# Two streamed weight granules of the last projection phase, 41 and 44, trade places with their neighbours 42 and 45

## The chip, the cores and the metric

The kernel runs on one core of a Trainium2 chip. The metric is the device time of one execution in microseconds (us); of several executions the median is given. Beside the times there is one profiled execution, whose page and trace are quoted here. Engines are called as the profile calls them: PE is TensorE, DVE is VectorE, ACT is ScalarE, POOL is GpSimd, SP is SyncE.

## The reference: what is computed

The input x is 2048 rows of 1024 values in bfloat16. It is normalised row by row (xn), and the output is x plus two terms.

The first term is a recurrent attention. The 2048 rows are cut into 64 segments of 32 rows. Each segment is put behind an 8-row memory, so 40 rows go through q, k and v projections (1024 to 32 heads of 128), masked softmax attention and the output projection:

```python
h = jnp.concatenate([mem, xs], axis=1)          # 8 memory rows, 32 rows of the segment
q = jnp.einsum('btd,dhe->bhte', h, Wq)          # likewise k and v
...
o = jnp.einsum('bhte,hed->btd', o, Wo)
mem = o[:, :M, :].copy()                        # the memory of the next segment
outs.append(o[:, M:, :])
```

The memory of a segment is made by the one before it, so the segments run one after the other, and each needs all of Wq, Wk, Wv and Wo.

The second term is a router that picks two of the 2048 rows and runs them through a gated feed-forward layer (1024 to 3584 and back); the result is added to these two rows.

## The kernel before, in words

**Weights and granules.** The four matrices of the attention are cut into 64 granules of 128 x 2048 values (512 KB). Granules 0 to 47 belong to six projection phases of eight granules each, in the order of the list `PHASES` (L25): q and k of the first half of the heads, q and k of the second half, then v of the first half (granules 32 to 39) and v of the second half (granules 40 to 47). Granules 48 to 63 are the output projection. 44 granules stay resident on the chip; the other 20 are streamed from HBM again in every segment, each into one of five slots (`wstream`, `N_SLOT`, L19 and L97). Which ones are streamed is the list `streamed` (L74 to L80). In the kernel before it holds 2, 5, 6, 9, 13, 17, 21, 25, 29, 33, 36, 39, 41, 44, 47, 50, 53, 56, 59 and 62. After the first segment granule 6 is no longer read and only half of granule 25 is (the rest is kept in PSUM), so 19 reads remain per segment. In the first segment GpSimd copies the streamed granules to a scratch tensor in HBM (`wsc`), from which later segments read.

**The stream.** `fetch` (L318) issues the next read of a fixed list on SyncE's queue; later segments use the line L327. It needs a free slot, so SyncE waits until TensorE has finished with the slot's last content. Fetches are issued in order, five granules ahead: what frees a slot is that all matmuls of a streamed granule are done, and `after` (L434), called at that point of the program, issues the next fetch. So the end of streamed granule number n in the list is followed by the fetch of number n + 5: the end of 41 by the fetch of 56, the end of 44 by that of 59.

**The order of work.** The order on each engine is written out by hand; no scheduler changes it. Per segment TensorE runs the six phases (loop at L650), in each phase the eight granules in order, each with four matmuls 128*32 by 512 columns (L668, tile `PSm`). Between granules stand hooks, small pieces of other work tied to a phase and a granule: the transposes of the projections, `scores` (L527), the softmax on ScalarE and VectorE, and `attend` (L571, matmuls at L583 and L585). The first `attend` of the first half stands behind the fifth granule of the last phase (granule 44), the second one behind the seventh (granule 46). ScalarE copies its result (L590 and L592). Then come the 16 granules of the output projection (`project`, L722), with the `attend` of the second half between them.

**The left rows.** The main pass of a segment takes 32 of its 40 rows: 24 of x and the 8 of the memory. The last 8 rows of x of four successive segments (a group) are handled together, as 32 left rows. Their projections are passes of their own over the same granules (`left_pass`, L644 to L647, tile `PSl`, four more matmuls per granule). They are spread over the group by j, the number of a segment in its group: in segments j = 1 and j = 2 those of q and k of the next group, in segments j = 0 those of v, in the two v phases; segments j = 3 have the output projection of the left rows (tile `WL`). Where the phase before had left passes too, the left passes of the first three granules of a phase are put behind the main pass of the fourth, and `after` is called behind the left pass:

```python
if PSl is None or kc >= 3 or not left_before:
    for g_, Gv_ in behind:
        if PSl is not None and g_ not in done and g_ not in later:
            left_pass(PSl, g_, Gv_, not done and g_ == rest[0], g_ == rest[-1])
        after(s, g_)
    behind = []
```

In segments j = 0 this concerns the second v phase, with granules 40, 41 and 42. For q and k of the second half the passes over resident granules are put off further (the list `later`); this does not apply to v.

**The rest.** GpSimd's queue carries the rows of x, the outputs and the left rows; ScalarE's queue stores the left projections (`ql_d`). At the end the weights of the feed-forward layer are read into the places of granules that are no longer needed (L371).

Of the kernel before, what the change touches and what calls it, by code (L numbers as in the profile page):

```python
# [17 lines left out]
N_RES = 44  # L18
N_SLOT = 5  # L19
KEPT_WHOLE = 6  # L20
KEPT_PART = 25
LEFT_OUT = 35
NEG = -30000.0

PHASES = [(0, 0), (1, 0), (0, 1), (1, 1), (2, 0), (2, 1)]  # L25
# [3 lines left out]
def kernel(  # L29
# [41 lines left out]


    NG = 64
    n_str = NG - N_RES  # L74
    streamed = [((2 * i + 1) * NG) // (2 * n_str + 2) for i in range(n_str + 1)]
    streamed.remove(LEFT_OUT)

    moved = {1: 2, 4: 5, 7: 9, 10: KEPT_WHOLE, 16: 17, 19: 21, 22: KEPT_PART, 25: 29, 28: 33, 32: 36, 38: 39}
    streamed = sorted(moved.get(g, g) for g in streamed)
    resident = [g for g in range(NG) if g not in streamed]  # L80

    def granule_dram(g):
# [417 lines left out]
    for s in range(NSEG):  # L500
# [149 lines left out]
        for p, (mat, half) in enumerate(PHASES):  # L650
# [13 lines left out]
            for kc in range(KC):  # L664
                g = 8 * p + kc
# [255 lines left out]
```

## Time and profile before

| | |
|---|---|
| Runs of the kernel before | 1920.88, 1941.53 and 1932.7 us, median 1932.7 |
| The profiled execution's own time | 1935.58 us |
| Its span, first to last instruction | 1933.6 us |
| Mean granted TensorE clock in it | 0.957 of full speed |
| DMA packets | 712.42 MB, mean 368 GB/s |

The span is what the profile's shares refer to. A row of a group or of the timeline names a line of the kernel, an engine, an operation and the tile it writes, then `<-` and what it reads: `PSm<-g,ST` is a main matmul with a streamed granule (g) and the segment's rows (ST), `PSm<-wres,ST` one with a resident granule. A timeline row gives start and length in us, counts like instructions in a row (x4) and, in brackets, how long the engine had been idle before it and what ended that. The ends of matmuls are modelled and overlap the next ones, so the time that a granule takes is read from start to start. A row of a table by windows gives the stretch, its length, each engine's busy time and instructions, the granted clock, the share of DMA busy time and GB/s.

### The profile page before, as it was taken

Reading aid. Unit: us, or ns where it says so; the run is one execution under the profiler, and the core shown is the slowest. Engines: PE = TensorE matmul, PEld = TensorE weight load, DVE = VectorE, ACT = ScalarE, POOL = GpSimd, SP = SyncE. Lnnn points to the kernel's source line nnn. Section 1 sums busy time; section 2 is a strip of 40 time slices with the busy share of each in tenths; the row PEclk is TensorE's granted clock in tenths of the full one; section 3 lists DMA queues with packets and bytes.
Section 4 is the critical chain, followed back from the end, with each engine's and each line's share of the span. In section 5 each row is a group of like instructions: output and inputs, shape, how many; then the busy total and the mean of one; then the engine's idle time right before and its main releaser. Section 6 shows DMA issues by size and latency. Waiting matters only on the chain.

```text
span 1933.6 us, 82883 instructions
## 1 busy us (share of the span) xinstructions
PE 1619.9 (84%) x36080; PEld 883.4 (46%) x36080; DVE 887.4 (46%) x2848; ACT 721.0 (37%) x1931; POOL 439.9 (23%) x882
## 2 busy tenths in 40 slices
PE   3558898989889898989999898988889898988874
PEld 1224444445444444445454444545444554545443
DVE  6734543554444445444454454444444444345430
ACT  1124343444434343433444343443434343344320
POOL 3211212222221312222131221222131222212120
PEclk8669999999999999999999999999999999999985
DMA  9999999999999999999999999999999999999998
GB/s 369 408 356 379 344 375 352 378 376 362 379 330 387 367 372 388 355 371 341 379 375 379 370 382 358 357 389 357 378 362 368 377 370 373 352 382 362 375 370 334
DMA packets 232123, 712.42 MB, mean 368 GB/s; under 512 B 39296, under 2 KB 53168, under 8 KB 231760
## 3 DMA queue, kind: packets, MB, share of 16 engines
q1 hardware_dynamic: 194384, 671.18, 92.3%
q0 software_dynamic: 28736, 28.09, 4.4%
q10 hardware_dynamic: 8640, 7.87, 1.2%
q8 instruction: 282, 4.62, 0.9%
q14 instruction: 81, 0.66, 0.1%
HBM read 694.32 MB, written 22.29 MB: 371 GB/s over the span
## 4 chain that ended last, share of the span: by engine, by line
PE 45%; DMA 44%; DVE 4%; ACT 3%; issue 3%; SPq 0%; ACTq 0%; POOL 0%; POOLq 0%; DVEq 0%
DMA g<-wsc 38%; PE PSm L668 22%; PE WO L722 7%; PE PSl L646 4%; PE BT L515 3%; PE WL L722 3%; ACT OTL L592 1%; PE BT L465 1%; DMA MW<-in_B_w_gate_dram 1%; DVE XR L227 1%; DMA MW<-in_B_w_up_dram 1%; DMA g<-in_A_Wq_dram 1%; DMA wres<-in_A_Wo_dram 1%; PE BS L583 1%; ACT QT L520 1%
## 5 line engine op out<-in xcount | busy, mean ns | idle before, releaser
L668 PE MATMUL PSm<-wres,ST 128*32 128x512 bf16 x8448 | 720.1, 386 | 18.2 <-DVE ST L282 6.7
L668 PEld LDWEIGHTS <-ST 128*32 128x32 bf16 x12288 | 324.1, 96 | 418.1 <-issue 191.3
L668 PE MATMUL PSm<-g,ST 128*32 128x512 bf16 x3588 | 365.5, 387 | 97.0 <-DMA g<-wsc 78.3
L684 ACT CAST XB<-PSm 128x512 bf16<-128x512 f32 x256 | 149.8, 585 | 293.8 <-PE PSm L668 292.3
L722 PEld LDWEIGHTS <-OT 128*32 128x32 bf16 x8192 | 202.4, 97 | 105.4 <-issue 84.5
L722 PE MATMUL WO<-wres,OT 128*32 128x256 bf16 x5632 | 231.9, 277 | 18.9 <-issue 9.6
L458 POOL DMA_DIRECT2D LX<-ql_d x63 | 33.5, 532 | 876.4 <-DVE OTL L592 350.8
L646 PE MATMUL PSl<-wres,STL 128*32 128x512 bf16 x2112 | 196.6, 390 | 2.5 <-issue 1.6
L525 DVE COPY KT<-BT 128x512 bf16<-128x512 bf16 x128 | 52.5, 410 | 313.7 <-ACT XB L684 134.5
L252 POOL DMA_DIRECT2D XN<-in_A_x_dram x256 | 128.5, 507 | 242.1 <-DMA out_dram<-XN 106.4
L786 POOL DMA_DIRECT2D out_dram<-XN x256 | 129.1, 513 | 222.0 <-DVE XN L784 216.1
L722 PE MATMUL WO<-g,OT 128*32 128x256 bf16 x2560 | 131.3, 279 | 37.3 <-DMA g<-wsc 29.2
L706 ACT CAST VM<-PSm 128x512 bf16<-128x512 f32 x128 | 79.7, 623 | 123.1 <-PE PSm L668 123.1
L520 ACT COPY QT<-BT 128x512 bf16<-128x512 bf16 x128 | 74.9, 585 | 113.0 <-PE BT L515 111.9
L646 PEld LDWEIGHTS <-STL 128*32 128x32 bf16 x3072 | 85.0, 98 | 63.9 <-issue 11.5
L350 ACT COPY BK<-KEPT 128x512 bf16<-128x512 bf16 x126 | 78.3, 621 | 90.8 <-PE WO L722 90.8
L354 DVE COPY g<-KEPT 128x512 bf16<-128x512 bf16 x126 | 47.7, 420 | 129.9 <-PE PSm L668 65.4
L515 PEld LDWEIGHTS <-XB 128*128 128x128 bf16 x1024 | 58.6, 98 | 106.5 <-ACT XB L684 75.7
L583 PEld LDWEIGHTS <-VM 32*128 32x128 bf16 x2048 | 69.5, 91 | 74.7 <-issue 67.4
L515 PE MATMUL BT<-IDENT,XB 128*128 128x128 bf16 x1024 | 102.2, 223 | 1.4 <-ACT QKL L476 1.4
L542 DVE TENSOR_TENSOR BS<-BS,CT 128x96 f32<-128x96 f32 (+1 forms) x256 | 59.7, 233 | 93.0 <-PE BS L535 88.5
L784 DVE CAST XN<-WO 128x256 bf16<-128x256 f32 x64 | 27.2, 425 | 152.3 <-PE WO L722 152.3
(170 smaller groups left out, 2457.3 us busy)
## 6 DMA issues: line engine op xcount, KB each, us to landing
g<-wsc SPq DMA_DIRECT2D x1134, 512.0 KB, 6.1
g<-wsc SPq DMA_DIRECT2D x63, 256.0 KB, 5.4
LX<-ql_d POOLq DMA_DIRECT2D x63, 128.0 KB, 6.1
ql_d<-XBl ACTq DMA_DIRECT2D x60, 128.0 KB, 5.8
MW<-in_B_w_gate_dram SPq DMA_DIRECT2D x16, 448.0 KB, 9.5
MW<-in_B_w_up_dram SPq DMA_DIRECT2D x16, 448.0 KB, 9.0
wres<-in_A_Wk_dram SPq DMA_DIRECT2D x12, 512.0 KB, 12.0
MW<-in_B_w_down_dram SPq DMA_DIRECT2D x12, 512.0 KB, 10.2
```

What stands on the lines that cost most here:

```text
L252: nc.gpsimd.dma_start(out=XN[32 * g:32 * g + XM, :], in_=x2[s * SEG:s * SEG + XM, 256 * g:256 * (g + 1)])
L350: copy(out=back[c][:, :], in_=KEPT_COLS[KEPT_WHOLE][c])
L515: nc.tensor.transpose(out=PTq[:, il, :, :].rearrange("p j r -> p (j r)"), in_=XB[:, il * P:(il + 1) * P], identity=IDENT[:, :])
L520: nc.scalar.copy(out=QT[half][:, :, :], in_=pv)
L542: nc.vector.tensor_tensor(out=S4, in0=S4, in1=m, op=ALU.add)
L583: nc.tensor.matmul(o, lhsT=VM[half][q0:q0 + 32, il * P:(il + 1) * P], rhs=PTm[q0:q0 + 32, il, 0:NK], start=True, stop=False, tile_position ...
L646: nc.tensor.matmul(PSl[32 * jq:32 * jq + 32, :], lhsT=STL[:, g % KC, :], rhs=part(Gv, jq), start=first_, stop=last_, tile_position=(0, 32 ...
L668: nc.tensor.matmul(PSm[32 * jq:32 * jq + 32, :], lhsT=ST[:, kc, :], rhs=part(Gv, jq), start=(kc == 0), stop=(kc == KC - 1), tile_position= ...
L684: nc.scalar.copy(out=XB[:, :], in_=PSm[:, :])
L706: nc.scalar.copy(out=VM[half][:, :], in_=PSm[:, :])
L722: nc.tensor.matmul(PS[32 * g:32 * g + 32, 0:256], lhsT=lhs(h), rhs=Gv[:, D * hs + 256 * g:D * hs + 256 * (g + 1)], start=False, stop=(last ...
L786: nc.gpsimd.dma_start(out=out2[s * SEG:s * SEG + XM, 256 * g:256 * (g + 1)], in_=OB[32 * g:32 * g + XM, :])
```

## The change

The list of streamed granules is written out, and two entries differ: 42 and 45 take the place of 41 and 44. Granules 41 and 44 become resident, 42 and 45 streamed. The number of streamed granules, the five slots, the hooks and the order of the passes stay, the left passes in the v phases too. The other entries are the same as before.

```diff
-LEFT_OUT = 35
...
-    n_str = NG - N_RES
-    streamed = [((2 * i + 1) * NG) // (2 * n_str + 2) for i in range(n_str + 1)]
-    streamed.remove(LEFT_OUT)
-
-    moved = {1: 2, 4: 5, 7: 9, 10: KEPT_WHOLE, 16: 17, 19: 21, 22: KEPT_PART, 25: 29, 28: 33, 32: 36, 38: 39}
-    streamed = sorted(moved.get(g, g) for g in streamed)
+
+    streamed = [2, 5, KEPT_WHOLE, 9, 13, 17, 21, KEPT_PART, 29, 33, 36, 39, 42, 45, 47, 50, 53, 56, 59, 62]
+    assert len(streamed) == NG - N_RES
+    n_str = len(streamed)
     resident = [g for g in range(NG) if g not in streamed]
```

## The prediction

> **What bounds the kernel now.** I read the page first, then the waits, then the windows of one group of four segments, then TensorE's timeline in the second v phase (granules 40 to 47) of segments of each kind.
>
> ```profile
> span 1933.6 us, 82883 instructions
> PE 1619.9 (84%) x36080; PEld 883.4 (46%) x36080; DVE 887.4 (46%) x2848; ACT 721.0 (37%) x1931; POOL 439.9 (23%) x882
> q1 hardware_dynamic: 194384, 671.18, 92.3%
> HBM read 694.32 MB, written 22.29 MB: 371 GB/s over the span
> PE 45%; DMA 44%; DVE 4%; ACT 3%; issue 3%; SPq 0%; ACTq 0%; POOL 0%; POOLq 0%; DVEq 0%
> g<-wsc SPq DMA_DIRECT2D x1134, 512.0 KB, 6.1
> ```
>
> The chain that ended last is shared almost evenly by TensorE and by the streamed granules (g<-wsc). Neither is the bound everywhere; the places where they change over decide what an edit is worth. The waits between the two, over the whole kernel (us in total, times, longest):
>
> ```profile
> PE PSm L668 <- DMA g<-wsc: 78.3, 158, 2.3
> PE WO L722 <- DMA g<-wsc: 29.2, 81, 1.3
> ```
>
> So all of TensorE's waiting for the stream is 107.5 us, some 1.7 us in each of 63 segments: an order of the stream can hardly bring more than that. The windows below are the four segments 32 to 35 (j = 0, 1, 2, 3), cut at the first main matmul of each; j = 2 is cut in three, j = 0 and j = 3 in two. The last two columns are the DMA share and GB/s.
>
> ```profile
> 993.53:1007.50 13.97, 13.97 (x322) 7.51 (x314) 5.37 (x15) 5.31 (x11) 7.41 (x14) 1.00 0.97 338
> 1007.50:1020.21 12.71, 11.99 (x288) 6.53 (x284) 7.79 (x28) 6.60 (x21) 1.69 (x4) 1.00 1.03 400
> 1020.21:1047.12 26.91, 24.29 (x543) 13.51 (x539) 12.09 (x40) 11.22 (x30) 4.02 (x9) 1.00 1.01 381
> 1047.12:1052.00 4.88, 4.58 (x76) 2.11 (x72) 1.02 (x3) 1.17 (x2) 1.74 (x5) 1.00 1.03 384
> 1052.00:1059.50 7.50, 7.50 (x156) 3.57 (x156) 3.56 (x11) 4.08 (x9) 2.00 (x4) 1.00 0.98 338
> 1059.50:1073.89 14.39, 11.36 (x301) 6.90 (x293) 7.76 (x28) 6.00 (x20) 0.93 (x2) 1.00 1.03 403
> 1073.89:1091.00 17.11, 13.45 (x262) 6.20 (x263) 7.88 (x23) 5.95 (x12) 6.24 (x13) 1.00 0.99 361
> 1091.00:1101.95 10.95, 10.32 (x302) 7.50 (x305) 5.86 (x24) 4.24 (x16) 1.27 (x3) 1.00 0.97 363
> ```
>
> Where PE's busy time (third figure) equals the stretch, TensorE is the bound and the stream runs at 338 GB/s, held back by slots that come free late; elsewhere the stream is the bound, at 381 to 403 GB/s, and TensorE waits. Granules 41 and 44 stand at the end of a stream-bound stretch in j = 3 (1073.89 to 1091), and inside longer ones in j = 1 and j = 2. TensorE in j = 3, segment 35, from granule 39 to 47:
>
> ```profile
> 1088.63 0.40 PE L668 MATMUL PSm<-g,ST 128*32 128x512 bf16 x4 [0.65 <-DMA g<-wsc]
> 1088.84 0.40 PE L668 MATMUL PSm<-wres,ST 128*32 128x512 bf16 x4
> 1089.77 0.40 PE L668 MATMUL PSm<-g,ST 128*32 128x512 bf16 x4 [0.53 <-DMA g<-wsc]
> 1089.98 0.62 PE L668 MATMUL PSm<-wres,ST 128*32 128x512 bf16 x8
> 1090.99 0.40 PE L668 MATMUL PSm<-g,ST 128*32 128x512 bf16 x4 [0.39 <-DMA g<-wsc]
> 1091.33 0.19 PE L583 MATMUL WO<-PT,VM 32*128 32x40 bf16 x1
> 1091.62 0.62 PE L668 MATMUL PSm<-wres,ST 128*32 128x512 bf16 x8
> 1092.82 0.40 PE L668 MATMUL PSm<-g,ST 128*32 128x512 bf16 x4
> ```
>
> These are 39, 40, 41 (0.53 us idle before it), 42 with 43, 44 (0.39 idle), the first attend, 45 with 46, and 47, which does not wait. One granule is four matmuls, 0.21 to 0.22 us from start to start.
>
> **The change part by part.** It removes and adds no instruction: in the two built programs every engine has as many rows as before, and the order on DVE, ACT and POOL is the same. On TensorE the operand of 41 and 42, and of 44 and 45, trade places between a resident tile and a slot. On SyncE two resident loads of segment 0 read other rows. The bytes are equal. So each part is a matter of when TensorE meets a landing and when it gives a slot back.
>
> (1) Segments j = 3, 16 of them. The stream lands as before: 41's place in it becomes 42's, 44's becomes 45's. 41 is then done while TensorE waits. 42 starts at the landing, 1089.77; 43 and 44 follow at 1089.98 and, with the 0.12 us that the transition before 44 leaves, end near 1090.54; the first attend (0.29, 1091.33 to 1091.62) ends near 1090.83, so 45 waits 0.16 us for 1090.99. Before, 45 started at 1091.62. That is 0.63 us: the main pass of 44 and the attend, now inside the wait. Next late is 47. In this stretch landings that TensorE waits on come 1.22 us apart (1089.77, 1090.99), and 512 KB at the 403 GB/s of the window is 1.30, so 47 lands near 1092.25; TensorE would reach it at 1092.82 - 0.63 = 1092.19. I take 0.57 us. The wait that pays for it is there in other segments of this kind, 31 and 39:
>
> ```profile
> 980.72 0.40 PE L668 MATMUL PSm<-g,ST 128*32 128x512 bf16 x4 [0.78 <-DMA g<-wsc]
> 982.04 0.40 PE L668 MATMUL PSm<-g,ST 128*32 128x512 bf16 x4 [0.49 <-DMA g<-wsc]
> 1200.17 0.40 PE L668 MATMUL PSm<-g,ST 128*32 128x512 bf16 x4 [2.35 <-DMA g<-wsc]
> 1201.23 0.62 PE L668 MATMUL PSm<-g,ST 128*32 128x512 bf16 x4 [0.24 <-DMA g<-wsc]
> ```
>
> 16 x 0.57 = 9.1 us gained. The slots are given back no later here, since 42 and 45 start at the same landings as 41 and 44 did. Ends: 0 (if the stream stays the bound afterwards, for which the 0.97 share behind 1091 speaks) and 16 x 0.63 = 10.1.
>
> (2) Segments j = 1 and j = 2, 32 of them. The waits at 41 and 44 there, and those that follow in the same segment 33 (j = 1):
>
> ```profile
> 1036.39 0.40 PE L668 MATMUL PSm<-g,ST 128*32 128x512 bf16 x4 [0.43 <-DMA g<-wsc]
> 1042.86 0.40 PE L722 MATMUL WO<-g,OT 128*32 128x256 bf16 x8 [0.33 <-DMA g<-wsc]
> 1044.10 0.40 PE L722 MATMUL WO<-g,OT 128*32 128x256 bf16 x8 [0.18 <-DMA g<-wsc]
> 1045.32 0.40 PE L722 MATMUL WO<-g,OT 128*32 128x256 bf16 x8 [0.38 <-DMA g<-wsc]
> 1063.13 0.40 PE L668 MATMUL PSm<-g,ST 128*32 128x512 bf16 x4 [0.24 <-DMA g<-wsc]
> ```
>
> The 0.43 at 44 in j = 1 and the 0.24 in j = 2 go, but the next three waits come 1.22 to 1.24 us apart, which is the stream's own pace: TensorE arrives earlier and waits longer. Value 0. Ends: the whole of the waits gained, 16 x (0.43 + 0.24) = 10.7 us; or a loss, since 45 now starts without a wait some 0.2 us behind its landing, and its slot goes back that much later: 32 x 0.2 = 6.4.
>
> (3) Segments j = 0, 16 of them, where each granule has a left pass too (L646), and in the second v phase those of the first granules stand behind the main pass of the fourth. Segment 32:
>
> ```profile
> 1009.33 0.62 PE L646 MATMUL PSl<-wres,STL 128*32 128x512 bf16 x8
> 1010.18 0.40 PE L646 MATMUL PSl<-g,STL 128*32 128x512 bf16 x4
> 1011.04 0.39 PE L646 MATMUL PSl<-wres,STL 128*32 128x512 bf16 x4
> 1016.69 0.40 PE L722 MATMUL WO<-g,OT 128*32 128x256 bf16 x8
> DMA to landing us min/median/max: 4.2/5.9/7.2
> ```
>
> The left pass of 42 is the first half of the row at 1009.33, right behind 41's: that slot goes back 0.22 us later. 44's slot went back behind the row at 1010.18, 45's goes back behind that at 1011.04: 0.86 us later. SyncE's queue holds nothing but the next fetches, in order; behind the late one stands granule 62's, which waits for 47's slot anyway. The late fetch is granule 59's, used at 1016.69: from 1010.57 to there are 6.1 us, and would be 5.3. Its median landing of 5.9 says 0.6 us of wait; but at the 400 GB/s of that window a granule takes 1.31 us, so 5.2 us of the landing is this transfer and the three ahead of it, and a fetch that joins the queue later finds it shorter. I take a loss of 0.1 us, 1.6 in all; ends 0 and 16 x 0.6 = 9.6.
>
> Nothing in segment 0 and in the expert part is priced: two loads there trade places with equal bytes.
>
> Sum: -9.1 + 0 + 1.6 = -7.5 us on the profiled execution's 1935.58 (its span and 2.0 around it). The median of the three runs is 1932.7, 0.15% below that; I take the difference from the median: 1925.
>
> [...]
>
> **The rivals.** *The stream is the bound throughout.* The DMA share is 0.97 to 1.03 in all windows, even where TensorE is the bound; then an earlier TensorE in j = 3 only waits longer in j = 0. Against it: no wait for the stream in segment 32's v phases, and 47 in j = 3 doesn't wait. Gain 0: 1933.
>
> *Late slots starve the stream, slower.* The place is granule 59 in j = 0 (and 45's slot in j = 1, 2). It decides if the landing follows the issue and not the queue: then 0.6 us a group and the 6.4 of part 2, with nothing from part 1: 9.6 + 6.4 = 16 us, 1949. For it: the stream fell to 338 GB/s where slots came late. Against: fetches there landed in as little as 4.2 us.
>
> *More is gained.* If the hidden waits of j = 1 and j = 2 also bring later fetches forward, the stream gains what TensorE gains: 9.1 + 10.7 = 19.8 us, 1913.
>
> That the change does not do what it says is excluded by the instruction order.
>
> **How the numbers follow.** The forecast (1918 to 1930) has 0.5, no gain 0.2, slower 0.13, more 0.17. Three runs of one kernel spread over 20 us, so about 1% is what a measurement tells from no change. More gain lands on either side of 1%; so faster by over 1% has 0.19, slower by over 1% 0.11 (the upper part of its rival and the spread), within 1% 0.70. The range reaches from just under the larger gain, 1908, to most of the slower case, 1943.
>
> **What would show it.** In j = 3, TensorE's waits stand before 42 and 45 and are together some 0.3 us shorter, 47 begins to be met at its landing, and the segment is 0.5 us shorter. In j = 1 and j = 2 the waits at L722 grow by what goes at 45. In j = 0 a wait before 59 of more than 0.2 us would show part 3 wrong. If j = 3 is shorter and j = 0 or j = 1 longer by as much, the stream is the bound. The prediction is wrong if landings move, by fetches issued at other times or by transfers beside them, more than TensorE's order does.

## The result and the profile after

Over 20 runs each, the changed kernel's median is 1924.72 us (1919.29 to 1934.03) and that of the kernel before 1931.01 (1920.88 to 1946.21); the ratio is 0.9961, with a 95% interval of 0.9945 to 0.9977. By the medians that is 6.3 us, 0.33%; by the ratio, which is not that of the two medians, it is 0.39%, or 7.5 us of 1931. The profiled execution took 1926.78 us.

The page of the changed kernel, the lines that answer to those shown of before:

```profile
span 1924.8 us, 82883 instructions
PE 1614.6 (84%) x36080; PEld 889.6 (46%) x36080; DVE 886.7 (46%) x2848; ACT 721.8 (38%) x1931; POOL 439.9 (23%) x882
q1 hardware_dynamic: 194384, 671.18, 92.6%
HBM read 694.32 MB, written 22.29 MB: 372 GB/s over the span
DMA 47%; PE 43%; DVE 3%; ACT 3%; issue 2%; SPq 1%; ACTq 0%; POOL 0%; DVEq 0%; POOLq 0%
g<-wsc SPq DMA_DIRECT2D x1134, 512.0 KB, 6.1
```

Instructions and bytes are the same, the span is 8.8 us shorter. The lines of the kernel are three lower than before: L665 is the main matmul, L719 the output projection, L580 the attend. TensorE's waits after, in the view of waits (us in total, times, longest):

```profile
PE PSm L665 <- DMA g<-wsc: 67.8, 127, 1.5
PE WO L719 <- DMA g<-wsc: 28.5, 88, 0.9
PE WO L580 <- ACT OTL L589: 22.4, 29, 1.0
```

and the one of before that the third answers to:

```profile
PE WO L583 <- ACT OTL L592: 8.8, 20, 0.8
```

The waits for the stream in the phases fell by 10.5 us, those in the output projection stayed, and TensorE's wait for ScalarE's copies of an attend grew by 13.6 us.

Where the time went is read from the windows view, by cutting the same stretch out of every segment of a kind. Each row below is the sum line of such a query: the length of all stretches together, then each engine's busy time in them. First the kernel before. In this order: granule 40 to granule 47 of the 16 segments j = 3; granule 47 to 56 of the same; granule 40 to the end of the segment in the 16 segments j = 1, in the 16 segments j = 2, and in 15 segments j = 0.

```profile
sum 73.26, PE 49.36 PEld 21.39 DVE 60.66 ACT 28.38 POOL 0.00; mean PE 3.09 PEld 1.34 DVE 3.79 ACT 1.77 POOL 0.00
...
sum 69.54, PE 66.25 PEld 44.04 DVE 36.41 ACT 26.61 POOL 0.00; mean PE 4.14 PEld 2.75 DVE 2.28 ACT 1.66 POOL 0.00
...
sum 204.71, PE 167.52 PEld 101.16 DVE 109.57 ACT 91.30 POOL 15.26; mean PE 10.47 PEld 6.32 DVE 6.85 ACT 5.71 POOL 0.95
...
sum 200.04, PE 154.53 PEld 94.27 DVE 106.79 ACT 91.52 POOL 14.93; mean PE 9.66 PEld 5.89 DVE 6.67 ACT 5.72 POOL 0.93
...
sum 190.23, PE 171.74 PEld 95.60 DVE 112.74 ACT 98.59 POOL 16.90; mean PE 11.45 PEld 6.37 DVE 7.52 ACT 6.57 POOL 1.13
```

The same five of the changed kernel:

```profile
sum 64.17, PE 46.43 PEld 21.36 DVE 52.15 ACT 30.61 POOL 0.00; mean PE 2.90 PEld 1.33 DVE 3.26 ACT 1.91 POOL 0.00
...
sum 75.45, PE 70.82 PEld 46.08 DVE 41.74 ACT 24.76 POOL 0.00; mean PE 4.43 PEld 2.88 DVE 2.61 ACT 1.55 POOL 0.00
...
sum 201.47, PE 166.05 PEld 101.97 DVE 109.54 ACT 91.33 POOL 15.27; mean PE 10.38 PEld 6.37 DVE 6.85 ACT 5.71 POOL 0.95
...
sum 202.01, PE 155.84 PEld 95.78 DVE 106.39 ACT 91.82 POOL 14.96; mean PE 9.74 PEld 5.99 DVE 6.65 ACT 5.74 POOL 0.94
...
sum 192.08, PE 172.28 PEld 98.83 DVE 113.24 ACT 98.73 POOL 17.77; mean PE 11.49 PEld 6.59 DVE 7.55 ACT 6.58 POOL 1.18
```

The first pair is the gain: 73.26 to 64.17, 9.1 us in the last v phase of j = 3. The second pair takes 5.9 of it back just behind (a second profile of the same kernel, in the experiments, takes back only 1.9). The other three move by -3.2, +2.0 and +1.9 us. Together that is -2.6 us, while the span fell by 8.8, so two more stretches are needed: granule 40 to the end of the segment in 15 segments j = 3 (all but the last), and the start of the segment to granule 40 in 15 segments j = 0. The kernel before, then the changed kernel:

```profile
sum 215.08, PE 178.49 PEld 119.03 DVE 118.87 ACT 78.52 POOL 24.36; mean PE 11.90 PEld 7.94 DVE 7.92 ACT 5.23 POOL 1.62
sum 233.17, PE 219.43 PEld 120.05 DVE 83.48 ACT 79.62 POOL 116.69; mean PE 14.63 PEld 8.00 DVE 5.57 ACT 5.31 POOL 7.78
...
sum 210.34, PE 179.53 PEld 120.79 DVE 115.65 ACT 79.01 POOL 22.88; mean PE 11.97 PEld 8.05 DVE 7.71 ACT 5.27 POOL 1.53
sum 228.56, PE 217.27 PEld 119.08 DVE 82.61 ACT 79.61 POOL 116.87; mean PE 14.48 PEld 7.94 DVE 5.51 ACT 5.31 POOL 7.79
```

From granule 40 to their end, the segments j = 3 are 4.7 us shorter (8.0 in the second profile, which has 207.06 there): half of the phase's gain or more is still there when the segment ends. The 4.6 us in j = 0 can't be put down to the change: the kernel with 42 alone (below), which is no faster than the kernel before, has 225.81 in that stretch. The profiled execution of the kernel before lies 4.6 us above the median of its runs, that of the changed kernel 2.1 above.

The timeline of TensorE in segment 35 (j = 3) after, from the passes of 40 and 41 to granule 47; rows of the attends are left out:

```profile
1081.60 0.40 PE L665 MATMUL PSm<-g,ST 128*32 128x512 bf16 x4 [0.88 <-DMA g<-wsc]
1081.82 0.62 PE L665 MATMUL PSm<-wres,ST 128*32 128x512 bf16 x8
...
1082.82 0.40 PE L665 MATMUL PSm<-g,ST 128*32 128x512 bf16 x4
1083.03 0.40 PE L665 MATMUL PSm<-wres,ST 128*32 128x512 bf16 x4
...
1085.19 0.40 PE L665 MATMUL PSm<-g,ST 128*32 128x512 bf16 x4 [1.25 <-DMA g<-wsc]
```

The wait stands before 42 (0.88 us idle); 43, 44 and the first attend follow, and 45 starts at 1082.82, 1.22 us behind 42, without an idle time that the view shows. Then 47 waits, 1.25 us here: the next late one. In this length segment 35, on which the prediction was worked out, is an exception: from 40 to 47 it takes 5.08 us here and took 3.98 before. Segment 51 shows the usual case, again 42, 45 and 47:

```profile
1524.23 0.40 PE L665 MATMUL PSm<-g,ST 128*32 128x512 bf16 x4 [0.62 <-DMA g<-wsc]
...
1525.45 0.40 PE L665 MATMUL PSm<-g,ST 128*32 128x512 bf16 x4
...
1526.68 0.40 PE L665 MATMUL PSm<-g,ST 128*32 128x512 bf16 x4
```

From 45 to 47 are 1.23 us. In the kernel before, 44 to 47 took 1.83 us (1090.99 to 1092.82 in the prediction's rows). In the timeline of the 15 segments j = 3 from segment 7 on, that distance is 1.83 or 1.84 us in 12 before, and 1.14 to 1.23 us in 10 after. The 0.6 us between them are the pass of 44 and the first attend, which now stand ahead of the landing of 45.

### The profile page after: what moved, and what is told of

The parts are those of the page before. It is cut to its first block, busy times and chain, and to the rows that moved or that the text cites. A ratio compares the mean times of both kernels' runs of the same rounds, so it can differ in the third digit from the quotient of the medians.

```text
span 1924.8 us, 82883 instructions
## 1 busy us (share of the span) xinstructions
PE 1614.6 (84%) x36080; PEld 889.6 (46%) x36080; DVE 886.7 (46%) x2848; ACT 721.8 (38%) x1931; POOL 439.9 (23%) x882
## 4 chain that ended last, share of the span: by engine, by line
DMA 47%; PE 43%; DVE 3%; ACT 3%; issue 2%; SPq 1%; ACTq 0%; POOL 0%; DVEq 0%; POOLq 0%
DMA g<-wsc 39%; PE PSm L665 21%; PE WO L719 7%; PE PSl L643 5%; PE BT L512 3%; PE WL L719 3%; DMA XP<-in_A_x_dram 2%; DMA out_dram<-XN 1%; PE BT L462 1%; DMA MW<-in_B_w_gate_dram 1%; DVE XR L224 1%; DMA MW<-in_B_w_up_dram 1%; ACT QT L517 1%; DMA g<-in_A_Wq_dram 1%; ACT XBl L691 1%
## 5 line engine op out<-in xcount | busy, mean ns | idle before, releaser
L665 PE MATMUL PSm<-wres,ST 128*32 128x512 bf16 x8448 | 716.1, 384 | 18.3 <-DVE ST L279 6.7
L665 PEld LDWEIGHTS <-ST 128*32 128x32 bf16 x12288 | 325.8, 96 | 385.0 <-issue 153.9
L665 PE MATMUL PSm<-g,ST 128*32 128x512 bf16 x3588 | 363.9, 387 | 89.1 <-DMA g<-wsc 67.8
L719 PEld LDWEIGHTS <-OT 128*32 128x32 bf16 x8192 | 208.3, 99 | 105.6 <-issue 81.2
L719 PE MATMUL WO<-wres,OT 128*32 128x256 bf16 x5632 | 239.4, 285 | 15.3 <-issue 7.9
L719 PE MATMUL WO<-g,OT 128*32 128x256 bf16 x2560 | 134.7, 286 | 38.8 <-DMA g<-wsc 28.5
L347 ACT COPY BK<-KEPT 128x512 bf16<-128x512 bf16 x126 | 78.3, 621 | 91.7 <-PE WO L719 91.7
L580 PEld LDWEIGHTS <-VM 32*128 32x128 bf16 x2048 | 68.7, 92 | 86.5 <-issue 79.0
```

What stands on the lines that cost most here:

```text
L347: copy(out=back[c][:, :], in_=KEPT_COLS[KEPT_WHOLE][c])
L580: nc.tensor.matmul(o, lhsT=VM[half][q0:q0 + 32, il * P:(il + 1) * P], rhs=PTm[q0:q0 + 32, il, 0:NK], start=True, stop=False, tile_position ...
L665: nc.tensor.matmul(PSm[32 * jq:32 * jq + 32, :], lhsT=ST[:, kc, :], rhs=part(Gv, jq), start=(kc == 0), stop=(kc == KC - 1), tile_position= ...
L719: nc.tensor.matmul(PS[32 * g:32 * g + 32, 0:256], lhsT=lhs(h), rhs=Gv[:, D * hs + 256 * g:D * hs + 256 * (g + 1)], start=False, stop=(last ...
```

## The experiments

All ratios are to the kernel before, run on the same chip, with 95% intervals. The **theory** is that of the prediction: the gain is work of TensorE (the pass of 44 and the first attend) that now stands inside the last wait of the stream-bound stretch of j = 3. The **rival** is that later granules or slots give the stream slack in all segments.

**One of the two swaps alone.**

```diff
-... 39, 42, 45, 47, ...
+... 39, 42, 44, 47, ...
```

> Streamed granules 42 and 44 (only the first of the two swaps). Theory (the gain is work of TensorE that stands inside the last wait of the stream-bound stretch of j = 3): the wait at 42 is 0.2 us shorter than the one at 41 was, but 44 still lands when it lands and TensorE starts it at that landing, so everything behind it is as before: ratio to the kernel before 1.000, within 0.002. Rival (any granule read later gives the stream slack in every segment): half of the change's gain for one of two swaps, ratio 0.998, and the waits of the whole kernel fall by some 4 us.

Measured: 1.0008 (0.9984 to 1.0033), median 1935.16 us. The sums for j = 3, granule 40 to 47, and 47 to 56:

```profile
sum 72.47, PE 49.19 PEld 22.04 DVE 60.12 ACT 29.29 POOL 0.00; mean PE 3.07 PEld 1.38 DVE 3.76 ACT 1.83 POOL 0.00
...
sum 80.98, PE 78.62 PEld 48.40 DVE 34.49 ACT 26.04 POOL 0.00; mean PE 4.91 PEld 3.02 DVE 2.16 ACT 1.63 POOL 0.00
```

The phase is as long as before (72.47 against 73.26): the first swap brings nothing there. TensorE's waits for the stream do not fall either, as the rival had them (82.1 us in the phases and 28.0 in the output projection, against 78.3 and 29.2 before).

```diff
-... 39, 42, 45, 47, ...
+... 39, 41, 45, 47, ...
```

> Streamed granules 41 and 45 (only the second swap). Theory: TensorE does 42, 43, 44 and the first attend between the landings of 41 and 45 (1.22 us apart, that work takes some 1.27), so 45 starts at most 0.05 us behind its landing in j = 3 and 0.58 us earlier than before: 16 x 0.57 = 9 us less the 1.6 of j = 0, ratio 0.996, the whole of the change's gain. Rival (slack in the stream, shared by both swaps): ratio 0.998.

Measured: 0.9969 (0.9945 to 0.9992), median 1927.52 us. The same two sums:

```profile
sum 65.31, PE 46.53 PEld 20.79 DVE 53.42 ACT 30.75 POOL 0.00; mean PE 2.91 PEld 1.30 DVE 3.34 ACT 1.92 POOL 0.00
...
sum 71.24, PE 66.36 PEld 44.12 DVE 43.52 ACT 24.87 POOL 0.00; mean PE 4.15 PEld 2.76 DVE 2.72 ACT 1.55 POOL 0.00
```

65.31 stands beside the 64.17 of both swaps. The second swap carries the gain. The intervals of the two kernels overlap a little, from 0.9984 to 0.9992, and the one with 42 alone ran at a lower mean clock (0.949 against 0.953), so the times alone do not part them for certain. The rival that gives each swap half falls with the phase sums.

**The attends moved, in both kernels.**

```diff
-        hook(5, 4, lambda: attend(0, 0))
+        hook(5, 5, lambda: attend(0, 0))
...
-        hook(5, 6, lambda: attend(0, 1))
+        hook(5, 7, lambda: attend(0, 1))
```

> The changed kernel with both attends of the first half one granule later (behind 45 and 47 in place of 44 and 46); nothing is left out. Theory: in j = 3 the first attend (0.29 to 0.41 us) no longer stands inside the wait for 45, and the second one (0.58) no longer inside that for 47, so the last phase of j = 3 is some 0.5 us longer and 47 waits some 0.45 us: 8 us slower than the changed kernel, ratio to the kernel before 1.000. Rival (what counts is when the slots of 45 and 47 come free): they come free 0.4 to 0.6 us earlier in all 63 segments, so it is faster than the changed kernel, ratio 0.994 or less.

Measured: 1.0043 (1.0024 to 1.0062), median 1940.46 us, 16 us over the changed kernel's 1924.72 where 8 were expected. The sum from 47 to 56 in j = 3, which now holds the second attend too:

```profile
sum 93.35, PE 84.38 PEld 53.72 DVE 45.78 ACT 30.27 POOL 0.00; mean PE 5.27 PEld 3.36 DVE 2.86 ACT 1.89 POOL 0.00
```

That is 18 us more than in the changed kernel, of which the moved attend is 16 x 0.58 = 9.3. The expectation left out a wait. With the second attend behind granule 47, TensorE waits for ScalarE's copies of it at the start of the output projection (L711); this kernel first, then the changed one:

```profile
PE WO L711 <- ACT OTL L589: 34.7, 64, 0.5
...
PE WO L711 <- ACT OTL L589: 6.0, 31, 0.2
```

That is some 0.54 us in each segment, 8.7 us in the 16 of j = 3. The clock was lower too, 0.947 on the mean of the 12 timed runs against 0.954 of the kernel before. The sign is the theory's: slots that come back earlier in all segments do not make this kernel faster. But the experiment brings a cost of its own, so that the attends' place outside the waits is the price is not shown by it.

```diff
-        hook(5, 4, lambda: attend(0, 0))
+        hook(5, 3, lambda: attend(0, 0))
...
-        hook(5, 6, lambda: attend(0, 1))
+        hook(5, 5, lambda: attend(0, 1))
```

> The kernel before (41 and 44 streamed) with both attends one granule earlier (behind 43 and 45); nothing is left out. Theory: in j = 3 the first attend now stands inside the wait for 44 and the second inside that for 47, with no granule traded: 47 is met 0.4 us earlier, 16 x 0.4 = 6 us, ratio 0.997; if TensorE has to wait for the VectorE or ScalarE results that the attend reads in the other segments, less. Rival (slots and the place of granules in the stream decide): no granule or slot moves, so the ratio is 1.000.

Measured: 0.9991 (0.9970 to 1.0011), median 1928.84 us. In its profile the phase of j = 3 is as short as in the changed kernel, with no granule traded, while TensorE's wait for ScalarE's copies rose from 8.8 us to 22.8:

```profile
sum 64.33, PE 46.15 PEld 20.64 DVE 52.70 ACT 32.54 POOL 0.00; mean PE 2.88 PEld 1.29 DVE 3.29 ACT 2.03 POOL 0.00
...
PE WO L583 <- ACT OTL L592: 22.8, 30, 1.1
```

So the work inside the wait is enough to shorten that phase, but the time can't be told from no change: the expected 0.997 is the end of the interval. Of the 8.9 us gained there, 4.9 are lost in the same phase of the other segments (j = 1: 71.61 before, 72.27 here; j = 2: 68.90 and 73.11), as the expectation's last condition allows. This one is inconclusive for the whole kernel.

**One granule further.**

```diff
-... 39, 42, 45, 47, ...
+... 39, 42, 46, 47, ...
```

> Streamed granules 42 and 46: one granule further than the change. Theory: in j = 3 another granule (0.22 us) goes into the wait, but 47 already starts at its landing in the changed kernel, so 46 and 47 wait in turn and nothing is gained there; the slot of 46 comes back 0.2 us later still: ratio 0.996 to 0.998. Rival (each granule further gives its own gain): 16 x 0.22 = 3.5 us more, 0.994.

Measured: 0.9959 (0.9936 to 0.9983), median 1924.69 us, the changed kernel's to 0.03. The sum from 40 to 47 in j = 3:

```profile
sum 61.94, PE 47.44 PEld 22.52 DVE 49.84 ACT 31.11 POOL 0.00; mean PE 2.97 PEld 1.41 DVE 3.11 ACT 1.94 POOL 0.00
```

That is 61.94 us; two profiles of the changed kernel itself gave 64.17 and 62.32 (below), so nothing of the rival's 3.5 us is seen beyond the scatter of the two. That agrees with 47's landing ending the stretch, as the prediction had it.

**Late slots in j = 0.**

```diff
-        hook(5, 4, lambda: attend(0, 0))
+        hook(5, 4 if j else 5, lambda: attend(0, 0))
...
-        hook(5, 6, lambda: attend(0, 1))
+        hook(5, 6 if j else 7, lambda: attend(0, 1))
```

> The changed kernel with both attends of the first half one granule later in the 16 segments j = 0 alone; nothing is left out. The slots of 45 and 47 come back 0.4 to 0.6 us earlier there, before the fetches of 59 and 62. Theory (part 3 of the prediction: 45's late slot costs little, 0.1 us a group, since the landing is set by the queue): 0 to 2 us gained, ratio 0.995 to 0.996. Rival (late slots starve the stream): the 0.4 us and more come back in each j = 0, 16 x 0.4 = 6 us, ratio 0.993 or less, and the waits for 56, 59 and 62 in j = 0 go.

Measured: 0.9957 (0.9927 to 0.9987), median 1924.69 us. Granule 40 to the end of 15 segments j = 0, and the wait for the stream in the output projection:

```profile
sum 191.12, PE 171.03 PEld 96.75 DVE 113.45 ACT 98.51 POOL 16.04; mean PE 11.40 PEld 6.45 DVE 7.56 ACT 6.57 POOL 1.07
...
PE WO L719 <- DMA g<-wsc: 24.3, 62, 1.6
```

Waits of 4.2 us go, and the stretch is 1.0 us shorter than the changed kernel's 192.08. As where the attends were moved in all segments, TensorE's wait at L711 grows, here from 6.0 to 13.9 us, so the 1.0 us is what the two leave. It agrees with the small price of part 3 and does not measure it; the 0.993 that starving would have given lies at the edge of the interval and is not excluded by the time alone.

**The clock.** In the changed kernel's profile the 5.9 us given back behind 47 go with something that no part of the prediction names. Two windows of it, one after the other, in segment 35:

```profile
1082.30:1085.70 3.40, 2.06 (x49) 1.11 (x45) 2.96 (x13) 1.74 (x10) 0.00 (x0) 1.00 1.01 407
1085.70:1089.10 3.40, 3.40 (x64) 1.92 (x65) 1.18 (x6) 0.52 (x1) 0.00 (x0) 0.50 0.99 396
```

In the first TensorE was busy for 2.06 of 3.40 us (the wait for 47 is in it); in the second its granted clock is 0.50. The stretch from 47 to 56 is 5.32 us long here and 4.09 in segment 47, at full clock:

```profile
1085.19:1090.51 5.32, 5.32 (x120) 3.23 (x119) 2.11 (x9) 1.06 (x3) 0.00 (x0) 0.68 0.98 370
...
1417.40:1421.49 4.09, 3.99 (x118) 2.70 (x117) 2.90 (x14) 1.57 (x7) 0.00 (x0) 1.00 1.05 424
```

What brings such a spell of half clock on is not shown; TensorE was 61% busy in the window before this one. To test whether the spells take the gain back, matmuls without a reader were put into the wait for 42:

```diff
+                if j == 3 and p == 5 and kc == 1:
+                    PSf = psL.tile([P, 512], F32, tag="accl", name="PSf")
+                    for i in range(2):
+                        for jq in range(4):
+                            nc.tensor.matmul(PSf[32 * jq:32 * jq + 32, :], lhsT=ST[:, kc, :], rhs=part(res_tiles[40], jq), ...)
```

> The changed kernel with eight added matmuls (two granules' worth, 0.43 us; their results are read by nobody) between 41 and 42 in the 16 segments j = 3, inside the wait for 42, which was 0.67 us idle on the mean of 14 segments. Theory on the clock: in the runs so far the granted TensorE clock fell to 0.50 for 3.4 us behind a stretch of j = 3 with much waiting (7 such spells of j = 3 in the changed kernel's profile, 4 in the kernel before, 11 with 42 alone), and j = 3 is 1.2 us longer where it did. The added work keeps the clock: spells of j = 3 fall to 3 or fewer and the kernel gains 4 to 5 us on the changed one, ratio to the kernel before 0.994. Rival (the spells only mark long waits and cost nothing by themselves, or eight matmuls don't prevent them): no gain, 0.996, or 0.997 where the added work isn't hidden.

Measured: 0.9956 (0.9929 to 0.9983), median 1922.43 us: a gain of 2 us on the changed kernel that its interval doesn't hold apart from none. So both were run again side by side:

> The changed kernel once more, to stand beside the next two on one chip: ratio to the kernel before 0.996, mean granted clock over the timed runs 0.950 to 0.952 (it was 0.951 over 20 runs, the kernel before 0.954 over 35).

> The changed kernel with the eight added matmuls behind 41 in j = 3 (results read by nobody), once more beside the changed kernel itself. Theory on the clock: mean granted clock 0.953 to 0.955 and 3 to 5 us less than the changed kernel beside it, ratio to the kernel before 0.994 to 0.9955. Rival (the added work changes the record of the clock and not the time): the same time as the changed kernel within 1.5 us.

Measured: the changed kernel again 0.9950 (0.9916 to 0.9984), median 1922.66 us, mean clock 0.952; with the filler 0.9951 (0.9920 to 0.9983), 1923.49 us, mean clock 0.954. The two sums for j = 3 (40 to 47, 47 to 56) of the changed kernel's second profile:

```profile
sum 62.32, PE 45.97 PEld 21.61 DVE 49.83 ACT 31.52 POOL 0.00; mean PE 2.87 PEld 1.35 DVE 3.11 ACT 1.97 POOL 0.00
...
sum 71.48, PE 66.03 PEld 44.28 DVE 44.44 ACT 24.01 POOL 0.00; mean PE 4.13 PEld 2.77 DVE 2.78 ACT 1.50 POOL 0.00
```

and with the filler:

```profile
sum 61.91, PE 53.95 PEld 25.87 DVE 49.69 ACT 30.23 POOL 0.00; mean PE 3.37 PEld 1.62 DVE 3.11 ACT 1.89 POOL 0.00
...
sum 68.17, PE 63.70 PEld 43.34 DVE 42.96 ACT 24.89 POOL 0.00; mean PE 3.98 PEld 2.71 DVE 2.68 ACT 1.56 POOL 0.00
```

The filler is hidden (61.91 against 62.32 with 8 us more PE work in it) and the stretch behind is 3 us shorter, but the time is the same. The spells of half clock in j = 3 are 2 with the filler and 3 in this second profile without it, so that it prevents them is not shown either. My theory that the clock takes back a good part of the gain falls: the 5.9 us of the first profile were in good part that execution's own (1.9 in the second one), and what the filler saves in j = 3 does not reach the end.

**Combinations.** With the second swap alone, the matmuls without a reader stand in its wait for 41, and there are three rounds of them; the first kernel has the late attends of j = 0 as well.

```diff
-... 39, 42, 45, 47, ...
+... 39, 41, 45, 47, ...
...
+                if j == 3 and p == 5 and kc == 0:
+                    PSf = psL.tile([P, 512], F32, tag="accl", name="PSf")
+                    for i in range(3):
...
-        hook(5, 4, lambda: attend(0, 0))
+        hook(5, 4 if j else 5, lambda: attend(0, 0))
...
-        hook(5, 6, lambda: attend(0, 1))
+        hook(5, 6 if j else 7, lambda: attend(0, 1))
```

> Streamed granules 41 and 45, twelve added matmuls (0.65 us, results read by nobody) between 40 and 41 in j = 3, and the attends one granule later in j = 0. If the gains of the three add up (45: -0.3%, clock -0.2%, slot in j = 0 -0.1%): ratio 0.994. If the clock and slot theories are wrong: 0.997, as 45 alone.

Measured: 0.9960 (0.9936 to 0.9984), median 1921.76 us.

The second is the same without the last two edits:

> Streamed granules 41 and 45 and twelve added matmuls between 40 and 41 in j = 3 (results read by nobody). If the second swap carries the gain and the added work keeps the clock: as the filler on the changed kernel, ratio 0.994 to 0.9955, granted clock 0.953 to 0.956. If the first swap matters too: 1 to 3 us more than that.

Measured: 0.9952 (0.9924 to 0.9980), median 1922.99 us. Neither can be told from the changed kernel; no version here is shown to beat it.

**What is late next in j = 1 and j = 2.** TensorE's wait for ScalarE's copies of an attend had grown by 13.6 us, where the waits for the stream in the phases fell by 10.5. Here ScalarE's copy and store of the left projection were put behind the attends' copies:

```diff
-                    hooks.setdefault((5, 2) if half else (p + 1, 0), []).append(store_ql)
+                    hooks.setdefault((5, 7) if half else (p + 1, 0), []).append(store_ql)
```

> The changed kernel with the copy and the store of the left projection (ScalarE, 0.59 us and 0.33 us of issue, segments j = 1 and j = 2) moved from the third granule of the last phase to its end, behind the copies of both attends; nothing is left out. In the changed kernel's profile TensorE waits 22.4 us for ScalarE's copies of the first attend (8.8 in the kernel before). Theory: in j = 1 and j = 2 the wait that went at 45 stands there now; with the copies first, that wait falls below 9 us. If the stream is the next bound in these segments, the waits for it grow by about as much and the time stays: ratio to the kernel before 0.995 to 0.997. Rival (ScalarE was the last thing in the way there): 10 us or more are gained, 0.991 or less.

Measured: 0.9920 (0.9894 to 0.9946), median 1923.26 us. TensorE's waits, then the sums for j = 1, granule 40 to 47 and 47 to the end:

```profile
PE PSm L665 <- DMA g<-wsc: 59.7, 123, 1.3
PE WO L719 <- DMA g<-wsc: 35.5, 81, 1.8
PE WO L719 <- issue: 17.8, 19, 1.8
...
sum 58.84, PE 52.64 PEld 28.36 DVE 46.82 ACT 30.22 POOL 0.00; mean PE 3.29 PEld 1.77 DVE 2.93 ACT 1.89 POOL 0.00
...
sum 144.66, PE 113.38 PEld 73.65 DVE 61.98 ACT 61.45 POOL 15.67; mean PE 7.09 PEld 4.60 DVE 3.87 ACT 3.84 POOL 0.98
```

and the same two sums of the changed kernel:

```profile
sum 69.35, PE 52.24 PEld 28.09 DVE 56.70 ACT 36.13 POOL 0.00; mean PE 3.27 PEld 1.76 DVE 3.54 ACT 2.26 POOL 0.00
...
sum 132.12, PE 113.81 PEld 73.87 DVE 52.84 ACT 55.20 POOL 15.27; mean PE 7.11 PEld 4.62 DVE 3.30 ACT 3.45 POOL 0.95
```

The wait of 22.4 us for the first attend's copies is gone (less than 0.4 us is left), the phase is 10.5 us shorter over the 16 segments, and the stretch behind it is 12.5 us longer, with the same PE work: all of it is taken back. The waits for the stream in the output projection grew by 7.0 us over the whole kernel (28.5 to 35.5), those for which the profile shows no releaser (`issue`) by 8.0 (9.8 to 17.8). So the stream is seen to take back about half, and what takes the rest stays open. The ratio is lower than the expected 0.995 to 0.997, and the rival's 0.991 lies within its interval. But the median is that of the changed kernel run again (1922.66), the kernel before beside it was slower than in the other batches (1935.59), and the intervals of this kernel and the changed one touch; a gain on the changed kernel is not shown, nor is it excluded.

## Why the prediction was right, and where a step was not

**Part 1 (j = 3, 9.1 us gained)** was right in size and in cause, for the phase itself. It lost 9.1 us by the first profile of the changed kernel and 10.9 by the second; the second swap alone does it, the first alone does not. The step is the one forecast: 45 is met 1.2 us ahead of 47 where 44 was met 1.83 us ahead of it. That 9.1 was met to the digit is luck: the 0.57 us were taken from segment 35, whose stretch from 40 to 47 got longer, and a segment's 40 to 47 scatters by more than that. That 47 is the next late one, and caps the gain, agrees with its wait in segment 35, and with a further granule in the wait that brought no more. How much of it reaches the end is less sure: the segment was to be 0.5 us shorter, and from 40 to its end it is 0.3 by the first profile and 0.5 by the second. With the attends moved in place of the granules the phase was as short, and the time could not be told from that of the kernel before.

**Part 2 (j = 1 and j = 2, value 0)** was right in size: -3.2 and +2.0 us. Its step "TensorE arrives earlier and waits longer" at the output projection failed: these waits did not grow (29.2 to 28.5 us). What is late next is ScalarE's copies of the first attend, on which the second attend waits (8.8 to 22.4 us). Only with that wait taken away did the waits for the stream there grow, by 7.0 us. So the bound I named is there, one behind the bound that I did not name.

**Part 3 (j = 0, 1.6 us lost)** is not settled. The stretch is 1.9 us longer in the first profile of the changed kernel and 1.1 us shorter in the second (189.17 against 190.23), and the experiment that gave the slots back earlier moved another wait with them. The place that the prediction watches behaves as it says: in TensorE's timeline of 15 segments j = 0 the waits before 59 add up to 0.2 us before, and to 1.0 and 1.6 in the two profiles of the changed kernel; one and two of the 15 are over 0.2 us.

The sum, -7.5 us, stands beside -6.3 by the medians and -7.5 by the ratio. Of the rivals, "the stream is the bound throughout" agrees with j = 1 in the last experiment, where a phase shorter by 10.5 us gave nothing to the end of the segment, and falls for j = 3, where half of it or more stayed. "Late slots starve the stream" has no support: the kernel is faster. "More is gained" failed at the same place as the step in part 2.

What stays open is how much of the phase's 9 to 11 us is given back where: the two profiles of the changed kernel differ by 4.0 us in the stretch behind 47 (75.45 and 71.48), and spells of half clock touch five of its 16 stretches in the first and one in the second.

## What to carry to other kernels

Where a stream and an engine take turns as the bound, read each stretch for the wait that ends last, and put into exactly that wait work that is ready; moving an earlier wait of the same stretch brought nothing here (1.0008). Where something else is late right behind, a wait that was removed came back there: in j = 1 first at ScalarE's copies, and then, with those out of the way, in the output projection (10.5 us gone, 12.5 back). Price a move by what is ready to stand inside the wait (here one granule's pass and one attend, 0.63 us), not by the length of the wait.

## What was not expected of the hardware

TensorE's granted clock fell to 0.50 for a 3.4 us window right behind a window in which it was 61% busy, in the middle of a kernel that keeps it busy for 84% of its span. Of the 16 stretches behind 47 in j = 3 such spells touched two in the profile of the kernel before, five in the changed kernel's first, one in its second and ten with 42 alone; the mean clock over that last kernel's 12 timed runs was 0.949, against 0.954 for the kernel before beside it.
